# Dealing the steps of a prepared projection anew among the last slots of an attention loop

## The chip, the cores and the metric

The kernel runs on one core of a Trainium2 chip. A core has TensorE (PE; its weight loads are counted apart as PEld), VectorE (DVE), ScalarE (ACT), GpSimd (POOL) and SyncE (SP), whose queue issues nearly all transfers (DMAs) here. The metric is the device time of one execution in microseconds (us), the median of several. Beside it stands one execution recorded by the profiler. The kernel is a long one of some 1.37 milliseconds, with 36,810 recorded instructions.

## The reference

Four residual layers, A, B, A, B, on one sequence of 2048 rows of 512 numbers, in float32, with 32 heads of 16:

```python
def _A_ref(x, wqkv, w_phi, wo):          # linear attention with a softmax feature map
    q, k, v = ...                        # x @ wqkv, by heads
    phi_q, phi_k = ...                   # softmax(q @ w_phi) and softmax(-(q @ w_phi)), joined; k likewise
    kv = einsum("bhsf,bhsd->bhfd", phi_k, v); z = einsum("bhsf->bhf", phi_k)
    return (phi_q @ kv / (phi_q @ z + 1e-6)) @ wo

def _B_ref(x, wq, wk, wv, wo, beta):     # causal softmax attention in 4 segments of 512 rows, and a memory
    for s in range(4):
        p = softmax(qs @ ks.T * scale + mask)          # qs, ks, vs: segment s of q, k, v
        a_dot = p @ vs
        a_mem = phi(qs) @ M / (phi(qs) @ z + 1e-6)     # phi(t) = t + 1 where t > 0, else exp(t)
        outs.append(g * a_mem + (1 - g) * a_dot)       # g = sigmoid(beta)
        M, z = M + phi(ks).T @ vs, z + phi(ks).sum()
    return concat(outs) @ wo

x = x + _A_ref(layernorm(x), ...)        # twice: A, then B
x = x + _B_ref(layernorm(x), ...)
```

## The kernel before

**Precision.** Most matmuls split each factor into a high and a low part (the names end in h and l, so oh and ol are the parts of a transposed attention output o) and add up three products: high with high, high with low, low with high.

**The loop of a layer B.** `LayerB.steps` works off 32 half chunks: 4 segments, 4 chunks of 8 heads, and the two halves of a chunk. A half chunk has R = 5 slots, 0 to 4, so that "slot 7.3" is slot 3 of the eighth half chunk of a segment. The loop runs once per layer B. In each slot TensorE computes one piece of the attention scores (`attend`; tile lg, one buffer of two banks), ScalarE its exponential (tile P), and GpSimd masks the diagonal of P. Up to slot 6.0 of the last segment TensorE also computes the scores' maxima for a later half chunk (`maxima`; tiles mx, my, g). At slot 0 of the next half chunk `weighted` multiplies the probabilities with the values into g, and ScalarE copies the result to U; `finish` transposes U and weighs it into tmp or ot.

**The tables.** What else a slot does stands in a table of text: FIRST and GAPS for the segments 0 to 2, and for the last segment LAST in the first layer B and FINAL in the second. "7.2 P/5 v/1" means: in slot 7.2 take five steps of P and one of the work that follows the loop. A slot's own scores (and maxima) stand on TensorE ahead of what the table puts there. Within each engine instructions keep the order in which the program emits them (`held`, `Ordered`).

**P, the prepared projection.** `early` computes the output projection of the last segment for the first three of the four chunks, before the fourth is known: once for rows 0 and 1 of four blocks of 128 rows (slots 6.2 to 6.4), once for rows 2 and 3 (7.1 onward). "pre" loads the residual, "pt" transposes (o into oh and ol), and P takes steps of `mm3_pair`. What is left when the loop ends is run behind it, partly before `end_turn` transposes the last chunk and partly after; `end` then adds the fourth chunk's products and stores the result.

**`mm3_pair`.** It works two outputs at a time. TensorE's array is used as two halves of 64 rows; a step is two matmuls side by side, one per half, for two different banks (po). With three chunks there are 9 products, and the steps are dealt in three parts of 4, 9 and 5: steps 0 to 3, 4 to 12 and 13 to 17. Between two parts the row halves exchange the banks that they write. So that two halves do not write one bank at once, an empty instruction on SyncE's queue waits for the last matmul of the part, and the first matmul of the next part waits for that instruction. This is a handover; there are two per call, ahead of step 4 and of step 13. (With four chunks, as in Q, V and O, the parts have 6, 12 and 6 steps, and the tables deal those by sixes.)

**Buffers.** oh and ol have OO = 2 buffers each: the pair for rows 2 and 3 and then the pair of `end_turn`. So the parts that `end_turn` makes overwrite what the last steps of P read.

The order of TensorE is thus set by the tables alone. In LAST, slots 7.2 to 7.4 also hold "v", steps of the next layer A (a K projection: g<-e,hh and g<-e,hl).

Of the kernel before, what the change touches and what calls it, by code (L numbers as in the profile page):

```python
# [18 lines left out]
P = 128  # L19
# [60 lines left out]
3.0 max turn turn fin ln | 3.1 O/6     | 3.2 O/6           | 3.3 O/6 | 3.4 O/6  # L80
4.0 max ln ln a2 fin a2 | 4.1 v/2      | 4.2 v/2           | 4.3 v/2 | 4.4 v/2
5.0 max a3 a3 fin | 5.1 v/2           | 5.2 v/2           | 5.3 v/2 | 5.4 v/2
6.0 max fin pre | 6.1 pt pt         | 6.2 P/6           | 6.3 P/6 | 6.4 P/6 v/1
7.0 max pt pt fin | 7.1 P/4           | 7.2 P/5 v/1       | 7.3 P/5 v/1 | 7.4 P/4 v/2
"""
FINAL = """
0.0 max a1 a1 fin | 0.1 Q2/6          | 0.2 Q2/6          | 0.3 Q2/6 | 0.4 Q2/6
# [2 lines left out]
3.0 max a2 a2 fin | 3.1 O/6           | 3.2 O/6           | 3.3 O/6 | 3.4 O/6  # L90
4.0 max turn turn fin | 4.1 O/6        | 4.2 O/6           | 4.3 O/6 | 4.4 O/6
5.0 max a3 a3 fin | 5.1 O/6           | 5.2 O/6           | 5.3 O/6 | 5.4 O/6
6.0 max fin pre | 6.1 pt pt         | 6.2 P/6           | 6.3 P/6 | 6.4 P/6
7.0 max pt pt fin | 7.1 P/4           | 7.2 P/3           | 7.3 P/3 | 7.4 P/2
"""
BEFORE = {-25: "load q0", -24: "sq0 sq1", -23: "k0", -22: "sk0 n n", -21: "sk1 v0/2 n n", -20: "v0/2 n n",
          -19: "n n", -18: "v1 n n", -17: "q1/2", -16: "q1/2", -15: "k1/2", -14: "k1/2", -12: "max0", -11: "v2"}
# [1458 lines left out]
```

## Time and profile before

| | us |
|---|---|
| median of 3 runs | 1367.28 |
| lowest and highest run | 1366.54, 1372.07 |
| the profiled execution | 1365.67 |
| its span, first to last instruction | 1363.9 |
| TensorE busy (share of the span) | 1316.8 (97%) |
| VectorE, ScalarE, GpSimd busy | 1040.8, 808.6, 696.9 |
| mean granted TensorE clock | 0.997 |

The two loops of layer B end at about 697 us and 1352 us of the span. How to read a row of the timeline: start and duration in us, engine, line of the program, operation, the tile written and the tiles read, shapes, the number of equal instructions that the row merges, and in brackets how long the engine had been idle before it and what released it. "<-SPq" is SyncE's queue, "<-issue" a wait for which the profile shows no cause. Line 176 holds all matmuls, line 180 all transposes, line 154 all instructions of the other engines, so rows are told apart by their tiles. The row w,oh or w,ol into g is a step of P, where the shape says 64 rows; e,e into lg are scores; P,v into g are weighted values.

### The profile page before, as it was taken

To read this page: it belongs to the slowest core of one execution; us is meant where nothing else is said; L and a number is where in the kernel's file an instruction comes from. 1 tells how busy PE (TensorE), PEld (TensorE's weight loads), DVE (VectorE), ACT (ScalarE), POOL (GpSimd) and SP (SyncE) were. 2 spreads that over 40 slices of the span, in tenths; PEclk is the share of its full clock that TensorE was granted. 3 is DMA by queue.
4 is the path that set the end of the run, shared out by engine and by line. 5 is a ranking of instruction groups with operands and counts; after the bars stand their busy time and mean duration, and the time that the engine had idled before them with its cause. 6 is when DMAs were issued, how large, how long until landed. Compare 5 with 4: busy or idle time off the path is not lost.

```text
span 1363.9 us, 36810 instructions
## 1 busy us (share of the span) xinstructions
PE 1316.8 (97%) x14056; PEld 1030.0 (76%) x14056; DVE 1040.8 (76%) x3256; ACT 808.6 (59%) x1201; POOL 696.9 (51%) x1060
## 2 busy tenths in 40 slices
PE   7999989999999999999999998999999999999997
PEld 6888868767777777777668886886777787787764
DVE  4776778778888888888647677787778879878882
ACT  5556345547677677677544433463666866866654
POOL 1568666326447557345324356553356656654442
PEclk9999999999999999999999999999999999999999
DMA  6388447535554545546251103755556554544441
GB/s 204 101 320 276 163 129 231 168 103 141 166 170 133 156 118 134 154 119 180 87 177 41 63 32 125 233 163 139 138 161 171 148 159 101 147 130 100 118 113 45
DMA packets 134400, 196.27 MB, mean 144 GB/s; under 512 B 15440, under 2 KB 61648, under 8 KB 133456
## 3 DMA queue, kind: packets, MB, share of 16 engines
q1 hardware_dynamic: 132256, 193.27, 48.5%
q8 instruction: 112, 1.84, 0.5%
q10 hardware_dynamic: 1968, 0.64, 0.2%
q14 instruction: 64, 0.52, 0.1%
HBM read 101.05 MB, written 39.85 MB: 103 GB/s over the span
## 4 chain that ended last, share of the span: by engine, by line
PE 75%; DVE 11%; ACT 5%; issue 4%; POOL 3%; DMA 2%; SPq 1%; DVEq 0%; ACTq 0%; POOLq 0%
PE g L176 57%; PE lg L176 6%; PE g L180 6%; PE mx L176 3%; ACT P L154 2%; DVE g L154 2%; PE lg L180 2%; POOL P L154 1%; PE my L176 1%; POOL tb L154 1%; DVE my L154 1%; DVE mx L154 1%; DVE mxs L154 1%; DVE es L154 1%; PE mx L180 1%
## 5 line engine op out<-in xcount | busy, mean ns | idle before, releaser
L154 ACT ACTIVATE P<-lg 128x1024 f32<-128x1024 f32 x320 | 329.6, 1030 | 170.9 <-PE lg L176 93.1
L154 POOL TENSOR_SCALAR_AFFINE_SELECT P<-P 128x256 f32<-128x256 f32 (+1 forms) x448 | 193.4, 446 | 293.1 <-ACT P L154 292.6
L154 DVE CUSTOM_DVE_ANT_0 g<-g,mask 128x256 f32<-128x256 f32 (+3 forms) x392 | 191.7, 545 | 9.6 <-PE g L176 9.4
L176 PE MATMUL g<-hh,wqk 64*128 64x512 f32 (+1 forms) x960 | 186.8, 393 | 0.0
L176 PE MATMUL g<-w,oh 64*128 64x512 f32 (+2 forms) x880 | 177.7, 384 | 1.3 <-DVE ol L154 0.7
L154 DVE CUSTOM_DVE_ANT_0 mx<-mx,mask 128x512 f32<-128x512 f32 (+2 forms) x316 | 157.9, 500 | 24.1 <-PE my L176 14.4
L154 DVE CUSTOM_DVE_ANT_0 my<-my,mask 128x512 f32<-128x512 f32 (+2 forms) x316 | 164.2, 519 | 0.0
L176 PE MATMUL lg<-e,e 64*128 64x256 f32 (+2 forms) x1024 | 153.0, 339 | 4.1 <-ACT P L154 4.1
L176 PE MATMUL g<-P,v 128*32 128x128 f32 (+3 forms) x2064 | 151.1, 433 | 4.9 <-DVE mxs L154 4.3
L176 PE MATMUL g<-w,hh 64*128 64x512 f32 (+1 forms) x672 | 143.7, 395 | 2.3 <-ACT w L154 1.3
L154 DVE DVE_READ_ACCUMULATOR2_ANT mxs<- 128x1 f32 x1024 | 145.8, 142 | 0.0
L176 PEld LDWEIGHTS lg<-e,e 64*128 64x128 f32 x1024 | 102.0, 185 | 35.2 <-issue 11.3
L176 PEld LDWEIGHTS g<-P,v 128*32 128x32 f32 x2064 | 61.3, 109 | 88.8 <-issue 62.4
L176 PEld LDWEIGHTS g<-w,oh 64*128 64x128 f32 (+1 forms) x880 | 106.9, 186 | 18.4 <-SPq L154 2.8
L176 PEld LDWEIGHTS g<-hh,wqk 64*128 64x128 f32 (+1 forms) x960 | 105.8, 185 | 16.5 <-PE mx L176 0.7
L154 POOL TENSOR_SCALAR tb<-tb 128x512 f32<-128x512 f32 x72 | 109.1, 1527 | 16.0 <-ACT tb L154 16.0
L176 PE MATMUL g<-w,ol 64*128 64x512 f32 (+2 forms) x440 | 115.6, 377 | 0.5 <-DVE ol L154 0.5
L176 PE MATMUL g<-hl,wqk 64*128 64x512 f32 (+1 forms) x480 | 106.3, 391 | 0.2
L154 ACT COPY tb<-g 128x512 f32<-128x512 f32 (+1 forms) x132 | 71.1, 576 | 48.5 <-PE g L176 46.7
L176 PEld LDWEIGHTS g<-w,hh 64*128 64x128 f32 (+1 forms) x672 | 84.3, 188 | 16.9 <-ACT w L154 1.6
L176 PE MATMUL g<-w,hl 64*128 64x512 f32 (+1 forms) x336 | 90.1, 393 | 0.0
L154 DVE TENSOR_REDUCE es<-P 128x64 f32<-128x1024 f32 x64 | 77.4, 1209 | 12.8 <-ACT P L154 12.8
(149 smaller groups left out, 2888.7 us busy)
## 6 DMA issues: line engine op xcount, KB each, us to landing
e<-ta SPq DMA_DIRECT2D x384, 128.0 KB
wqk<-wqk SPq DMA_DIRECT2D x128, 256.0 KB
x<-x SPq DMA_DIRECT2D x48, 256.0 KB
ot<-in SPq DMA_DIRECT2D x26, 256.0 KB
pq<-tb SPq DMA_DIRECT2D x24, 256.0 KB
tb<-pq SPq DMA_DIRECT2D x24, 256.0 KB
x<-xr SPq DMA_DIRECT2D x22, 256.0 KB
xr<-x SPq DMA_DIRECT2D x20, 256.0 KB
```

Of the source, the lines that this page charges most:

```text
L154: i = f(*a, **k)
L176: return held(nc.tensor.matmul(*a, **k))
L180: return held(nc.tensor.transpose(*a))
```

## The change

Only the two tables that hold P are changed. In slots 6.2, 6.3 and 6.4 the steps go from 6, 6, 6 to 4, 9, 5, in both loops. In 7.1 to 7.4 the first loop goes from 4, 5, 5, 4 to 4, 5, 4, 5; in the second it goes from 4, 3, 3, 2 with six steps behind the loop to 4, 5, 4, 0 with five behind it.

```diff
@@ LAST
-6.0 max fin pre | 6.1 pt pt         | 6.2 P/6           | 6.3 P/6 | 6.4 P/6 v/1
-7.0 max pt pt fin | 7.1 P/4           | 7.2 P/5 v/1       | 7.3 P/5 v/1 | 7.4 P/4 v/2
+6.0 max fin pre | 6.1 pt pt         | 6.2 P/4           | 6.3 P/9 | 6.4 P/5 v/1
+7.0 max pt pt fin | 7.1 P/4           | 7.2 P/5 v/1       | 7.3 P/4 v/1 | 7.4 P/5 v/2
@@ FINAL
-6.0 max fin pre | 6.1 pt pt         | 6.2 P/6           | 6.3 P/6 | 6.4 P/6
-7.0 max pt pt fin | 7.1 P/4           | 7.2 P/3           | 7.3 P/3 | 7.4 P/2
+6.0 max fin pre | 6.1 pt pt         | 6.2 P/4           | 6.3 P/9 | 6.4 P/5
+7.0 max pt pt fin | 7.1 P/4           | 7.2 P/5           | 7.3 P/4 | 7.4
```

The change moves instructions on TensorE only. On the other four engines they stand in the same order before and after, as do the transfers. The places, as differences (minus before, plus after):

TensorE in the second loop, slots 6.2 and 6.3, around the first handover (the row that waits for SP_sequencer); g_20164 and g_20165 are the two banks of the prepared projection, lg the scores of 6.3:

```order
 L176 MATMUL g_20164<-w_14902,oh_20139 128x512
 L176 MATMUL g_20165<-w_14902,oh_20141 128x512
+L176 MATMUL lg_20175<-e_2263_12760,e_2264_12761 128x256 [waits Activation_49]
+L176 MATMUL lg_20175<-e_2263_12760,e_2264_12761 128x256
+L176 MATMUL lg_20175<-e_2263_12760,e_2264_12761 128x384 x2
 L176 MATMUL g_20165<-w_14902,oh_20141 128x512 [waits SP_sequencer_49]
 L176 MATMUL g_20164<-w_14902,oh_20139 128x512
 L176 MATMUL g_20165<-w_14903,oh_20141 128x512
 L176 MATMUL g_20164<-w_14903,oh_20139 128x512
-L176 MATMUL lg_20179<-e_2263_12760,e_2264_12761 128x256 [waits Activation_49]
-L176 MATMUL lg_20179<-e_2263_12760,e_2264_12761 128x256
-L176 MATMUL lg_20179<-e_2263_12760,e_2264_12761 128x384 x2
```

The scores of 6.3 moved ahead of steps 4 and 5, so that they stand between step 3 and the handover's wait; at 6.3 and 6.4 the scores of 6.4 likewise moved behind step 12, ahead of the wait of step 13.

TensorE in the first loop, slots 7.3 and 7.4; e,hh and e,hl are the work of the next layer A, lg the scores of 7.4:

```order
 L176 MATMUL g_10448<-w_4966,ol_10418 128x512
 L176 MATMUL g_10447<-w_4966,ol_10416 128x512
-L176 MATMUL g_10447<-w_4967,oh_10415 128x512 [waits SP_sequencer_49]
-L176 MATMUL g_10448<-w_4967,oh_10417 128x512
 L176 MATMUL g_10480<-e_1902_10380,hh_9449 128x512 [waits DMAHW7_49]
 L176 MATMUL g_10480<-e_1903_10381,hh_9449 128x512 [waits DMAHW0_49]
 L176 MATMUL g_10480<-e_1902_10380,hl_9450 128x512
-L176 MATMUL lg_10513<-e_450_2824,e_451_2825 128x256 [waits Activation_49]
-L176 MATMUL lg_10513<-e_450_2824,e_451_2825 128x256 x3
+L176 MATMUL lg_10511<-e_450_2824,e_451_2825 128x256 [waits Activation_49]
+L176 MATMUL lg_10511<-e_450_2824,e_451_2825 128x256 x3
+L176 MATMUL g_10447<-w_4967,oh_10415 128x512 [waits SP_sequencer_49]
+L176 MATMUL g_10448<-w_4967,oh_10417 128x512
```

Step 13, the one that waits for the handover, moved from behind step 12 to behind the next layer's products and the scores of 7.4.

TensorE behind the second loop, around the transposes of the last chunk (L180; tmp is the last attention output). Behind the loop came steps 12 to 15, these transposes, 16 and 17; now come 13 to 16, the transposes, and 17:

```order
 L176 MATMUL g_20280<-w_14902,oh_20248 128x512
 L176 MATMUL g_20281<-w_14902,oh_20250 128x512
-L180 MATMUL g_20390<-ident,tmp_19924 128x128 [waits DVE_49,PE_49]
-L180 MATMUL g_20390<-ident,tmp_19924 128x128
-L180 MATMUL g_20397<-ident,tmp_19924 128x128 [waits DVE_49,PE_49]
-L180 MATMUL g_20397<-ident,tmp_19924 128x128
 L176 MATMUL g_20280<-w_14903,oh_20248 128x512
 L176 MATMUL g_20281<-w_14903,oh_20250 128x512
+L180 MATMUL g_20392<-ident,tmp_19924 128x128 [waits DVE_49,PE_49]
+L180 MATMUL g_20392<-ident,tmp_19924 128x128
+L180 MATMUL g_20399<-ident,tmp_19924 128x128 [waits DVE_49,PE_49]
+L180 MATMUL g_20399<-ident,tmp_19924 128x128
```

The transposes of the last chunk moved behind step 16, the last one that reads an oh buffer. Ahead of it steps 7 to 12 moved forward: slot 7.2 held steps 4 to 6 and now 4 to 8, slot 7.3 held 7 to 9 and now 9 to 12, slot 7.4 held 10 and 11 and now none.

## The prediction

> **What bounds the kernel now.** I read the page's first table, then its costliest groups for what ends the idle time of the weight loads (PEld), then the timeline of TensorE and ScalarE at the places of the change. The rows of the page:
>
> ```profile
> PE 1316.8 (97%) x14056; PEld 1030.0 (76%) x14056; DVE 1040.8 (76%) x3256; ACT 808.6 (59%) x1201; POOL 696.9 (51%) x1060
> ...
> L176 PEld LDWEIGHTS g<-w,oh 64*128 64x128 f32 (+1 forms) x880 | 106.9, 186 | 18.4 <-SPq L154 2.8
> ```
>
> TensorE is busy for 97% of the span, so what the change can win is TensorE's time. The second row is the output projection, of which the prepared one is a part: in the whole run its weight loads stood idle for 2.8 us until SyncE's queue spoke. That is the handover between the row halves. The order of instructions has 128 waits of TensorE on SyncE, and this 2.8 us is what the change is after; it is 0.2% of the span and sets the scale.
>
> In the last layer's loop, slots 6.2 to 7.0. First the weight load behind the first exposed handover (step 4, in slot 6.2), then TensorE from 6.4 on, then ScalarE's exponentials of 6.3, 6.4 and 7.0:
>
> ```profile
> 1335.60 0.19 PEld L176 LDWEIGHTS g<-w,oh 64*128 64x128 f32 x2 [0.53 <-SPq L154]
> ```
> ```profile
> 1336.17 0.46 PE L176 MATMUL lg<-e,e 64*128 64x256 f32 x4
> 1336.47 0.40 PE L176 MATMUL g<-w,ol 64*128 64x512 f32 x2
> ...
> 1337.87 0.45 PE L176 MATMUL lg<-e,e 64*128 64x256 f32 x4
> 1338.15 0.39 PE L176 MATMUL g<-w,ol 64*128 64x512 f32 x2
> 1338.65 0.50 PE L176 MATMUL g<-w,oh 64*128 64x512 f32 x2
> 1338.98 0.40 PE L176 MATMUL g<-w,ol 64*128 64x512 f32 x2
> 1339.22 0.63 PE L176 MATMUL g<-w,oh 64*128 64x512 f32 x4
> 1339.68 0.39 PE L176 MATMUL g<-w,ol 64*128 64x512 f32 x2
> 1339.91 0.40 PE L176 MATMUL lg<-e,e 64*128 64x512 f32 x2
> ```
> ```profile
> 1336.73 1.03 ACT L154 ACTIVATE P<-lg 128x1024 f32<-128x1024 f32 x1 [1.75 <-PE lg L176]
> 1338.42 1.03 ACT L154 ACTIVATE P<-lg 128x1024 f32<-128x1024 f32 x1 [0.66 <-PE lg L176]
> 1340.41 1.02 ACT L154 ACTIVATE P<-lg 128x1024 f32<-128x1024 f32 x1 [0.97 <-PE lg L176]
> ```
>
> Steps 14 to 17 start at 1338.98, 1339.22 (two of them) and 1339.68, so a step in flow takes 0.70 / 3 = 0.233 us. From step 12 (1338.15) over step 13 (1338.65) to step 14 (1338.98) it is 0.83 in place of 0.47: **an exposed handover costs TensorE 0.36 us**, 0.26 as a wait and 0.10 since the next weights come late. ScalarE waits for TensorE before each of the three exponentials, so TensorE sets the pace here.
>
> **The change part by part.** All five terms are of moved TensorE instructions; nothing is added or removed, and the order of the other engines and of SyncE's queue is the same before and after. So no transfer is moved past another; what SyncE has behind a handover only gets free sooner.
>
> *Slots 6.2 to 6.4, in both loops.* The scores (lg) of 6.3 now follow step 3. They no longer stand behind two steps (0.47) and the stall (0.36), so they start at 1336.17 - 0.83 = 1335.34. Steps 4 to 12 follow 0.30 later (1336.17 to 1336.47 above): nine steps, 2.10 us. The handover needs 0.50 from the last step's start (1338.15 to 1338.65), and the step and the scores between cover 0.23 + 0.30 = 0.53; only the late weights may show, so I add 0.06. The scores of 6.4 start at 1335.34 + 0.30 + 0.06 + 2.10 = 1337.80, just 0.07 sooner than the 1337.87 above. Steps 13 to 17, again behind scores (0.28 + 0.06), would let the scores of 7.0 start at 1337.80 + 0.34 + 5 x 0.233 = 1339.31, 0.60 sooner than 1339.91. But the exponential of 6.4 is only 0.07 sooner: it ends at 1338.42 + 1.03 - 0.07 = 1339.38, and there is one score buffer. So the scores start near 1339.44 with late weights (0.10): the gain is 1339.91 - 1339.54 = **0.37 us**, not 0.60. Bounds: 0, if the scores' cover is too short and ScalarE takes the rest, and 0.72, both stalls. I take 0.37, as ScalarE's rows stand nearest. Cover gone, each handover would cost its 0.36 again. What follows in 7.0 and 7.1 hangs on TensorE and passes this on. The first loop has the same two slots in the same order, and its part of the 2.8 us (six stalls of 0.47 on the mean, two each in these slots of both loops) says that they stall alike. So 0.37 twice.
>
> *Slot 7.3 of the first loop.* TensorE, where a piece of the next layer's K projection (g<-e,hh and hl; "v/1") follows the prepared steps 12 and 13:
>
> ```profile
> 692.21 0.39 PE L176 MATMUL g<-w,ol 64*128 64x512 f32 x2
> 692.70 0.50 PE L176 MATMUL g<-w,oh 64*128 64x512 f32 x2
> 693.13 0.73 PE L176 MATMUL g<-e,hh 128*128 128x512 f32 x2
> 693.70 0.40 PE L176 MATMUL g<-e,hl 128*128 128x512 f32 x1
> 694.02 0.52 PE L176 MATMUL lg<-e,e 64*128 64x256 f32 x4
> ```
>
> Step 13 moves behind the scores of 7.4. The handover is then covered by the K projection and the scores, over 1.2 us. A step followed by another kind of work takes about 0.32 (the second of the two steps at 1349.53 below starts at 1349.76, what follows at 1350.08), so the K projection starts at about 692.53, the scores at 693.42 in place of 694.02; the moved step (0.23) comes back in 7.4. Net **0.37 us**; bounds 0.26 (the wait alone) and 0.49 (692.70 less 692.21).
>
> *Slots 7.2 to 7.4 of the last loop.* TensorE in 7.2 and 7.4, then the mask (affine select) on the last probabilities:
>
> ```profile
> 1346.08 0.63 PE L176 MATMUL g<-w,oh 64*128 64x512 f32 x4
> 1346.54 0.40 PE L176 MATMUL g<-w,ol 64*128 64x512 f32 x2
> 1347.42 0.39 PE L176 MATMUL lg<-e,e 64*128 64x256 f32 x2 [0.48 <-ACT P L154]
> ```
> ```profile
> 1349.53 0.62 PE L176 MATMUL g<-w,oh 64*128 64x512 f32 x4
> 1350.08 2.37 PE L176 MATMUL g<-P,v 128*32 128x256 f32 x48
> ```
> ```profile
> 1350.90 0.64 POOL L154 TENSOR_SCALAR_AFFINE_SELECT P<-P 128x512 f32<-128x512 f32 x1 [0.94 <-ACT P L154]
> ```
>
> Here scores and exponential take turns at one buffer, and TensorE idles. From 1346.08 to 1347.42 there are 1.34 us; five steps take 1.17, so two more cost nothing (0.17 is left; with that cover gone, each further step costs 0.23). Slot 7.3 goes from three steps to four, with more to spare. Slot 7.4 loses its two steps, and the weighted sums need not wait until 1350.08. They are 48 instructions in 12 passes of four, about 0.2 each, and the last pass of all takes 0.4 to end. The last two passes read probabilities whose mask ends at 1350.90 + 0.64 = 1351.54, and they now start near 1350.08 + 2.37 - 0.4 - 0.2 = 1351.85. With 0.05 to 0.1 from mask to TensorE the gain is **0.2 us**, bounds 0 and 0.3.
>
> *Behind the last loop.* TensorE, ScalarE's cast and VectorE's low half:
>
> ```profile
> 1353.47 0.49 PE L176 MATMUL g<-w,ol 64*128 64x512 f32 x2
> 1354.07 0.50 PE L176 MATMUL g<-w,oh 64*128 64x512 f32 x2
> 1354.40 0.40 PE L176 MATMUL g<-w,ol 64*128 64x512 f32 x2
> 1354.63 0.39 PE L176 MATMUL g<-w,oh 64*128 64x512 f32 x2
> 1354.95 0.66 PE L180 MATMUL g<-ident,tmp 128*128 128x128 f32 x4
> 1355.54 0.50 PE L176 MATMUL g<-w,oh 64*128 64x512 f32 x2
> ```
> ```profile
> 1356.08 0.65 ACT L154 CAST oh<-g 128x256 fp32r<-128x256 f32 x2 [3.02 <-PE g L176]
> ```
> ```profile
> 1354.26 0.29 DVE L154 TENSOR_TENSOR tmp<-tmp,wt 128x128 f32<-128x128 f32 x1
> 1356.48 0.76 DVE L154 TENSOR_TENSOR ol<-g,oh 128x256 fp32r<-128x256 f32 x2 [1.93 <-ACT oh L154]
> ```
>
> Steps 12 to 15 stand at 1353.47 to 1354.63, the last transposes at 1354.95, then step 16, and 17 behind it. The cast writes the buffer (OO = 2) that step 16 reads: step 16 ends at 1355.54 + 0.50 = 1356.04, and the cast starts at 1356.08, though all four transposes had ended at 1354.95 + 0.66 = 1355.61. Afterwards four steps are left ahead of the transposes, 13 to 16: 1353.47, then 0.33 and twice 0.23 on, then 0.32 (1354.63 to 1354.95) to the transposes at 1354.59 (VectorE's tmp ends at 1354.55: just in time for the second pair). Step 17 follows 0.59 later (1354.95 to 1355.54 above) at 1355.18 and ends at 1355.68. The cast needs only its transposes, near 1355.1, so VectorE's low half, which overwrites what step 17 reads, starts at 1355.72 in place of 1356.48: **0.76 us**, more than the stall itself. Bounds 0.36 and 1.0. Everything behind it, to the last stores, hangs on it.
>
> Sum: 0.37 + 0.37 + 0.37 + 0.2 + 0.76 = 2.07, about 2.1 us. The profiled execution took 1365.67 (span 1363.9 and 1.8 around it), 1.6 below the median of 1367.28; it would come to 1363.6, and the median to 1365.2.
>
> **Rivals.**
>
> *The cover is too short (the change does not do what it says).* In 6.2 to 7.0 only 0.28 to 0.30 of scores stand in the border, and nine steps in 6.3 hold back the exponential of 6.4. If these slots win nothing in both loops, 1.33 is left: 1366.0. For it: the margin is 0.03 us. Against: even then the scores of 6.4 are not later than now.
>
> *The half clock.* In the second layer's first pass, the chain of waits and the windows around it:
>
> ```profile
> 836.85 2.23 issue
> ```
> ```profile
> 840.00:844.00 4.00, 4.00 (x12) 3.05 (x11) 3.93 (x7) 0.00 (x0) 2.33 (x3) 0.58 0.87 299
> ```
>
> TensorE waits 2.23 us for nothing that the trace names, and in the next 4 us its granted clock is 0.58, which costs 0.42 x 4 = 1.7 us. The first loop's 0.74 us moves the idle stretch; if the drop follows from where the stretch lies in a fixed grid, it can go, and the time is 1363.5. Against: nothing says so but one drop. [...]
>
> *One more such wait (slower).* The same "issue" wait, and the half clock behind it, cost 2.23 + 1.7 = 3.9 us. If moving TensorE's work by 0.74 us makes one more of them, say where the second layer's weights are loaded, the time is 1365.2 + 3.9 = 1369.1. It decides from 2.1 us on. For it: it is there once, in a stretch with DMA busy for 0.87. Against: instructions and transfers move together.
>
> **How the numbers follow.** The forecast has 0.55 (its own range, each term halfway to its bounds, is 1.3 to 2.7 us: 1364.6 to 1366.0). Too short a cover has 0.2, the clock 0.1, one more wait 0.1, other ways 0.05. The runs shown lie between 1366.54 and 1372.07, so 0.5% (6.8 us) is about what a measurement tells from no change. No case reaches it: same 0.95, slower 0.03, faster 0.02 for what no row shows. The range is 1361.8 to 1369.2: the clock's case less the forecast's spread, up to one more wait.
>
> **What would show it.** Right: no weight load of the output projection waits for SyncE; the scores of 6.3 start some 0.8 us sooner after those of 6.2, those of 6.4 about as now, and the exponential of 7.0 0.4 sooner; the cast behind the last loop starts ahead of step 17's end, and from the last U to the end the time is 0.8 shorter. Wrong: waits on SyncE of some 0.1 to 0.4 at 6.3 and 6.4, scores of 7.3 that come late behind five steps, or a last cast that waits as long as now.

## The result and the profile after

The changed kernel took 1362.78 us (median of 22 runs), the kernel before 1365.37 us beside it (22 runs): a ratio of 0.9974 with a 95% interval of 0.9963 to 0.9985, or 3.5 us less (2.0 to 5.0); the two medians by themselves lie 2.6 apart. Two of the changed kernel's 22 executions took 2557.12 and 4822.27 us, at a granted clock of 1.0; the ratio is without them, and why they took so long is open. The change is within 0.5%, as forecast, and by the ratio some 1.4 us more than the forecast 2.1. A later comparison of the same two kernels on one chip (below) gave 0.9989 (0.9973 to 1.0006), some 1.5 us less, with an interval that includes 1.

The profiled execution of the changed kernel took 1367.52 us, *more* than the 1365.67 of before. Its mean granted clock was 0.991, against 0.997, and its TensorE waited 0.50 and 0.53 us for SyncE at two places that the change does not touch (g<-hh,wqk, at 351.08 and 453.17). The changed places have to be read by themselves, then, as distances within one trace.

The page of the changed kernel, TensorE and the weight loads of the output projection:

```profile
PE 1320.3 (97%) x14056; PEld 1036.5 (76%) x14056; DVE 1041.6 (76%) x3256; ACT 808.2 (59%) x1201; POOL 695.2 (51%) x1060
...
L176 PEld LDWEIGHTS g<-w,oh 64*128 64x128 f32 (+1 forms) x880 | 108.9, 187 | 15.0 <-issue 1.5
```

The 2.8 us that these loads waited for SyncE's queue are gone: what ends most of their idle time is no longer "SPq", and the longer list of what they waited for in this trace does not name it.

The last loop, slots 6.2 to 7.0 in the changed kernel; TensorE at the two handovers, then ScalarE's exponentials of 6.2, 6.3, 6.4 and 7.0:

```profile
1337.98 0.73 PE L176 MATMUL g<-w,oh 64*128 64x512 f32 x2
1338.32 0.68 PE L176 MATMUL lg<-e,e 64*128 64x256 f32 x4
1338.80 0.73 PE L176 MATMUL g<-w,oh 64*128 64x512 f32 x4
...
1340.76 0.39 PE L176 MATMUL g<-w,ol 64*128 64x512 f32 x2
1340.99 0.40 PE L176 MATMUL lg<-e,e 64*128 64x256 f32 x4
1341.26 0.50 PE L176 MATMUL g<-w,oh 64*128 64x512 f32 x2
```
```profile
1337.13 1.04 ACT L154 ACTIVATE P<-lg 128x1024 f32<-128x1024 f32 x1
1339.09 1.03 ACT L154 ACTIVATE P<-lg 128x1024 f32<-128x1024 f32 x1 [0.92 <-POOL P L154]
1341.50 1.02 ACT L154 ACTIVATE P<-lg 128x1024 f32<-128x1024 f32 x1 [1.37 <-PE lg L176]
1343.17 1.02 ACT L154 ACTIVATE P<-lg 128x1024 f32<-128x1024 f32 x1 [0.65 <-PE lg L176]
```

Both handovers now have scores in them: from the last step (1340.76) over the scores (1340.99) to the next step (1341.26) is 0.50, the time that a handover took before, and TensorE works through it. The cover is only just as long as the handover. The row of 6.3 names GpSimd's mask (POOL P) as what released the exponential. The end of the scores, 1338.32 + 0.68 = 1339.00, explains its start as well: it comes 0.09 later, as in the kernel before (1336.17 + 0.46 = 1336.63, then 1336.73 at TensorE's release). Whether the mask too would hold it back is not shown. The kernel before had its exponential of 6.2 here, and its last U further on:

```profile
1333.94 1.04 ACT L154 ACTIVATE P<-lg 128x1024 f32<-128x1024 f32 x1
...
1352.58 0.47 ACT L154 ACTIVATE U<-g,share 128x256 f32<-128x256 f32 x1 [1.02 <-PE g L176]
```

From the exponential of 6.2 to those of 6.3, 6.4 and 7.0 it was 2.79, 4.48 and 6.47 us; it is 1.96, 4.37 and 6.04. So 6.3 comes 0.83 sooner, 6.4 only 0.11 and 7.0 0.43.

The first loop, slot 7.3 in the changed kernel: TensorE, where the next layer's K projection stands between step 12 and the scores of 7.4, then ScalarE's exponentials of 7.3 and 7.4 and its U behind the loop:

```profile
692.54 0.63 PE L176 MATMUL g<-w,oh 64*128 64x512 f32 x4
693.10 0.73 PE L176 MATMUL g<-e,hh 128*128 128x512 f32 x2
693.67 0.40 PE L176 MATMUL g<-e,hl 128*128 128x512 f32 x1
694.00 0.56 PE L176 MATMUL lg<-e,e 64*128 64x256 f32 x4
```
```profile
694.69 1.03 ACT L154 ACTIVATE P<-lg 128x1024 f32<-128x1024 f32 x1 [1.54 <-PE lg L176]
696.95 1.03 ACT L154 ACTIVATE P<-lg 128x1024 f32<-128x1024 f32 x1 [1.24 <-PE lg L176]
...
701.96 0.69 ACT L154 ACTIVATE U<-g,share 128x512 f32<-128x512 f32 x1 [2.57 <-PE g L176]
```

The same rows of the kernel before:

```profile
691.81 1.03 ACT L154 ACTIVATE P<-lg 128x1024 f32<-128x1024 f32 x1 [1.55 <-PE lg L176]
694.66 1.03 ACT L154 ACTIVATE P<-lg 128x1024 f32<-128x1024 f32 x1 [1.82 <-PE lg L176]
...
699.41 0.69 ACT L154 ACTIVATE U<-g,share 128x512 f32<-128x512 f32 x1 [2.32 <-PE g L176]
```

From 7.3 to 7.4 it was 2.85 and is 2.26; from 7.3 to U it was 7.60 and is 7.27.

The last weighted sums of the changed kernel: GpSimd's last mask, then the weight loads of the last passes:

```profile
1353.67 0.63 POOL L154 TENSOR_SCALAR_AFFINE_SELECT P<-P 128x512 f32<-128x512 f32 x1 [0.94 <-ACT P L154]
```
```profile
1354.36 0.16 PEld L176 LDWEIGHTS g<-P,v 128*32 128x32 f32 x8 [0.52 <-POOL P L154]
```

The mask ends at 1354.30, and these loads, now early, wait 0.52 for it; in the kernel before the 48 loads ran in one stretch of 1.89 us, from 1350.08 on.

Behind the last loop of the changed kernel: TensorE's transposes and step 17, ScalarE's last U and the cast, VectorE's low half:

```profile
1357.16 0.66 PE L180 MATMUL g<-ident,tmp 128*128 128x128 f32 x4
1357.74 0.50 PE L176 MATMUL g<-w,ol 64*128 64x512 f32 x2
```
```profile
1355.13 0.47 ACT L154 ACTIVATE U<-g,share 128x256 f32<-128x256 f32 x1 [1.16 <-PE g L176]
1357.63 0.65 ACT L154 CAST oh<-g 128x256 fp32r<-128x256 f32 x2 [2.03 <-PE g L180]
```
```profile
1358.35 0.76 DVE L154 TENSOR_TENSOR ol<-g,oh 128x256 fp32r<-128x256 f32 x2 [1.24 <-PE g L176]
```

The cast now waits for the transposes (line 180) and starts 2.50 behind the last U rather than 3.50. VectorE's low half waits for step 17 (line 176), no longer for the cast alone, and starts 3.22 behind the last U rather than 3.90. (In some traces of the same order, that of experiment 7 among them, its row names the cast, with 1.24 us of idle time as here; experiment 6 settles that it is the buffer.)

### The profile page after: what moved, and what is told of

It is laid out like the page before. It is cut to its first block, busy times and chain, and to the rows that moved or that the text cites. A ratio compares the mean times of both kernels' runs of the same rounds, so it can differ in the third digit from the quotient of the medians.

```text
span 1365.7 us, 36810 instructions
## 1 busy us (share of the span) xinstructions
PE 1320.3 (97%) x14056; PEld 1036.5 (76%) x14056; DVE 1041.6 (76%) x3256; ACT 808.2 (59%) x1201; POOL 695.2 (51%) x1060
## 4 chain that ended last, share of the span: by engine, by line
PE 74%; DVE 11%; ACT 4%; issue 4%; POOL 3%; DMA 2%; SPq 1%; DVEq 0%; ACTq 0%; POOLq 0%
PE g L176 56%; PE lg L176 6%; PE g L180 5%; PE mx L176 3%; ACT P L154 2%; PE lg L180 2%; POOL P L154 2%; DVE g L154 2%; SPq L154 1%; DVE es L154 1%; POOL tb L154 1%; PE my L176 1%; DVE my L154 1%; DVE mx L154 1%; DVE mxs L154 1%
```

## The experiments

Experiments 1 to 7 are one execution each, and their whole times, 1363.29 to 1367.30 us, tell nothing at this scale. Their expectations were written with the changed kernel's trace known, and quote it in places; what they left open was which part of the change does what. Their verdicts rest on six distances, each worked out from two starts in one trace (us). A: first loop, exponential of 6.2 to that of 7.0. B: first loop, exponential of 7.3 to U. C: as A, in the last loop. D: exponential of 7.0 to the last U. E: last U to the cast. F: last U to VectorE's low half. From there to the end it is 7.37 to 7.40 in every trace.

| | A | B | C | D | E | F |
|---|---|---|---|---|---|---|
| before | 6.48 | 7.60 | 6.47 | 12.17 | 3.50 | 3.90 |
| before, again | 6.47 | 7.63 | 6.47 | 12.17 | 3.50 | 3.90 |
| after | 6.34* | 7.27 | 6.04 | 11.96 | 2.50 | 3.22 |
| after, again | 6.04 | 7.27 | 6.04 | 11.95 | 2.50 | 3.21 |
| 1: slots 6.2 to 6.4 alone | 6.06 | 7.59 | 6.04 | 12.17 | 3.51 | 3.91 |
| 2: 7.2 to 7.4 of the last loop alone | 6.47 | 7.60 | 6.47 | 11.94 | 2.50 | 3.21 |
| 3: 7.3 and 7.4 of the first loop alone | 6.77* | 7.25 | 6.46 | 12.16 | 3.51 | 3.91 |
| 4: three steps in each of 7.2 to 7.4 | 6.37* | 7.24 | 6.03 | 12.40 | 2.50 | 3.21 |
| 5: before, free buffers | 6.77* | 7.59 | 6.46 | 12.17 | 2.86 | 3.26 |
| 6: after, free buffers | 6.05 | 7.25 | 6.04 | 11.94 | 2.50 | 2.90 |
| 7: 4, 6 and 8 steps | 6.12 | 7.27 | 6.13 | 11.94 | 2.50 | 3.22 |
| 8: free buffers, one step moved back | 6.05 | 7.27 | 6.04 | 11.95 | 2.26 | 2.67 |

The star marks stretches 0.29 to 0.33 longer than in the other traces of the same order. In that of "after" the granted clock was 0.50 for a part, from 678.31 to 681.73 (see the last section); I put the other three down to the same. Without those, one place repeats to within 0.05 us, mostly 0.02, whatever else was changed. So differences of 0.1 us can be told here, though the runs' times scatter by several us.

**1. Slots 6.2 to 6.4 alone.** The kernel before with one row of each table changed:

```diff
-6.0 max fin pre | 6.1 pt pt         | 6.2 P/6           | 6.3 P/6 | 6.4 P/6
+6.0 max fin pre | 6.1 pt pt         | 6.2 P/4           | 6.3 P/9 | 6.4 P/5
```

> Only the rows of slots 6.2 to 6.4 are changed (4, 9, 5 steps), in both loops. By the forecast's terms the scores of 6.3 come 0.83 us sooner after the exponential of 6.2, the exponential of 6.4 0.07 to 0.11 sooner, that of 7.0 0.37 to 0.43 sooner, in each loop; the slots 7.x and the work behind the last loop lie as before, so VectorE's low half (ol) still stands behind a cast that ends near where it did, and the whole is 0.7 to 0.9 us. Rival, the cover is too short: waits of the weight loads on SyncE of 0.1 to 0.4 us show at 6.3 and 6.4, and the exponential of 7.0 comes no sooner.

A and C fell by 0.42 and 0.43, all else stayed. ScalarE in the last loop (6.2, 6.3, 6.4, 7.0) and what ended the idle time of the weight loads:

```profile
1333.32 1.04 ACT L154 ACTIVATE P<-lg 128x1024 f32<-128x1024 f32 x1
1335.28 1.02 ACT L154 ACTIVATE P<-lg 128x1024 f32<-128x1024 f32 x1 [0.92 <-POOL P L154]
1337.69 1.02 ACT L154 ACTIVATE P<-lg 128x1024 f32<-128x1024 f32 x1 [1.38 <-PE lg L176]
1339.36 1.02 ACT L154 ACTIVATE P<-lg 128x1024 f32<-128x1024 f32 x1 [0.65 <-PE lg L176]
```
```profile
  SPq L154: 0.9, 2
```

Two long waits on SyncE are left, those at the first loop's 7.3 and behind the last loop. The scores do cover a handover, and the rival of too short a cover falls: the exponential of 7.0 comes 0.43 sooner with these rows alone.

**2. Slots 7.2 to 7.4 of the last loop alone.**

```diff
-7.0 max pt pt fin | 7.1 P/4           | 7.2 P/3           | 7.3 P/3 | 7.4 P/2
+7.0 max pt pt fin | 7.1 P/4           | 7.2 P/5           | 7.3 P/4 | 7.4
```

> Only the row of slots 7.2 to 7.4 of the last loop is changed (5, 4, 0 steps). By the forecast's terms the exponentials of 7.1 to 7.4 keep their distance to each other, the last weighted sums end 0.2 us sooner, the cast behind them starts a further 0.9 to 1.0 sooner and VectorE's low half (ol) 0.76 sooner (0.68 in the changed kernel), together 0.9 to 1.0 us to the end; the stalls in 6.2 to 6.4 stay. Rival, the gain behind the loop needs the earlier slots too (the steps there run later because 7.0 is later): under 0.5 us to the end.

D fell by 0.23, E by 1.00 and F by 0.69: 0.92 to the end, as expected, with the stalls of 6.2 to 6.4 still there. The gain does not need the earlier slots.

**3. Slots 7.3 and 7.4 of the first loop alone.** The LAST row of the change, 4 and 5 steps in place of 5 and 4.

> Only slots 7.3 and 7.4 of the first loop are changed (4 and 5 prepared steps). By the forecast's terms the scores and the exponential of 7.4 come 0.6 us sooner after those of 7.3, the moved step takes 0.23 back in 7.4, and what follows the loop is 0.37 us sooner (0.33 in the changed kernel). Rival, the moved step brings a new stall in 7.4 or the K projection waits for its own handover: 0.1 or less is left behind the loop.

The exponential of 7.4 came 2.25 behind that of 7.3 rather than 2.85, and B fell by 0.35. No new stall came with the moved step.

**4. Which steps stand ahead of the last weighted sums.** The changed kernel, with the same number left behind the loop:

```diff
-7.0 max pt pt fin | 7.1 P/4           | 7.2 P/5           | 7.3 P/4 | 7.4
+7.0 max pt pt fin | 7.1 P/4           | 7.2 P/3           | 7.3 P/3 | 7.4 P/3
```

> As the changed kernel, but the last loop's slots 7.2 to 7.4 hold 3, 3 and 3 steps in place of 5, 4 and none, so that the same four steps are left behind the loop and the same handover is avoided there. If the gain behind the loop comes from which step the cast waits for, the time from the last weighted sums to VectorE's low half is as in the changed kernel (0.7 us shorter than before); the three steps ahead of the weighted sums of 7.4 hold these back by one step more than before, 0.2 us later than before and 0.4 to 0.5 later than in the changed kernel. Rival, the weighted sums are bound by the mask of the last probabilities alone, wherever the steps stand: no later than in the changed kernel by more than 0.1.

E and F are those of the changed kernel, 2.50 and 3.21; D is 12.40, that is 0.23 later than before and 0.45 later than in the changed kernel. The rival, that the mask alone sets the weighted sums, falls. So the two parts come apart: the gain behind the loop comes from how many steps are left there, the gain in D from where the others stand. One more step ahead of the weighted sums costs one step, 0.23.

**5 and 6. Is it the buffer?** The parts of `end_turn` go to the buffers of ta1, which are free behind both loops, in the kernel before and in the changed one:

```diff
-    def turn(ot):
+    def turn(ot, tags=(("oh", OO), ("ol", OO))):
-        o = [T2("oh", OO, F32R), T2("ol", OO, F32R)]
+        o = [T2(tag, bufs, F32R) for tag, bufs in tags]
-            return [turn([last[:, t], last[:, t + 1]]) for t in (0, 2)]
+            return [turn([last[:, t], last[:, t + 1]], (("ta1", TA),) * 2) for t in (0, 2)]
```

> The kernel before, but the two parts of the result behind the last loop are written to free buffers (those of ta1) rather than to those of oh and ol that the prepared steps 16 and 17 still read; all steps stand as before. If it is the buffer that holds back the cast, it starts when its four transposes have ended: 0.5 to 0.65 us sooner after the last weighted sums than before, and VectorE's low half with it, whose wait is then for the cast alone; the exposed handover between steps 12 and 13 stays. Rival, the cast waits for TensorE's order and not for the buffer: nothing moves.

In the kernel before, with not one step moved, the last U, the cast and VectorE's low half:

```profile
1354.16 0.47 ACT L154 ACTIVATE U<-g,share 128x256 f32<-128x256 f32 x1 [1.02 <-PE g L176]
1357.02 0.65 ACT L154 CAST ta<-g 128x256 fp32r<-128x256 f32 x2 [2.39 <-PE g L180]
```
```profile
1357.42 0.76 DVE L154 TENSOR_TENSOR ta<-g,ta 128x256 fp32r<-128x256 f32 x2 [1.29 <-ACT ta L154]
```

The cast's wait is now for line 180, the transposes, and E and F fell by 0.64 each. The buffer was what held it back. Of the 1.00 that the change takes off E, 0.64 is the buffer; the other 0.36 (2.86 to 2.50 with free buffers, experiment 6) is the price of the handover that is no longer exposed.

> The changed kernel, but with the free buffers behind the last loop. In the changed kernel the cast starts at its transposes' end already, and VectorE's low half waits for step 17. Without that wait the cast lies as in the changed kernel, and VectorE's low half follows it 0.4 us after its start rather than 0.72: 0.3 us sooner to the end. Rival, the cast too still waited for step 16: then it comes sooner by some 0.1 to 0.3.

VectorE's low half in the changed kernel with free buffers:

```profile
1355.84 0.76 DVE L154 TENSOR_TENSOR ta<-g,ta 128x256 fp32r<-128x256 f32 x2 [0.93 <-ACT ta L154]
```

E stayed at 2.50 and F fell by 0.31 to 0.32, to 0.40 behind the cast. So in the changed kernel the low half's buffer still cost 0.3.

**7. Where the second handover lies.** The changed kernel with 4, 6 and 8 steps in slots 6.2 to 6.4 of both loops, which puts the second handover back inside slot 6.4.

> The changed kernel, but slots 6.2 to 6.4 of both loops hold 4, 6 and 8 steps rather than 4, 9 and 5. The first handover lies behind the scores of 6.3 as in the changed kernel, the second inside slot 6.4 as before (its wait of 0.4 to 0.5 on SyncE shows again). By the forecast's arithmetic the scores of 6.4 come three steps (0.7 us) sooner than in the changed kernel, the exponential of 6.4 as soon as ScalarE is free, and the scores of 7.0 stand behind all 18 steps and one stall: the exponential of 7.0 is 0.1 us later than in the changed kernel if TensorE sets it (0.83 of stalls less 0.36), or as in it. Rival, the exponential of 6.4 was what held up 7.0, so that bringing it forward by 0.7 us pays: the exponential of 7.0 is 0.2 us or more sooner than in the changed kernel.

The weight load behind that handover, then the exponentials of 6.4 and 7.0:

```profile
1337.25 0.19 PEld L176 LDWEIGHTS g<-w,oh 64*128 64x128 f32 x2 [0.53 <-SPq L154]
```
```profile
1336.57 1.03 ACT L154 ACTIVATE P<-lg 128x1024 f32<-128x1024 f32 x1 [0.68 <-PE lg L176]
1339.02 1.02 ACT L154 ACTIVATE P<-lg 128x1024 f32<-128x1024 f32 x1 [1.42 <-PE lg L176]
```

The stall is back, and A and C are 6.12 and 6.13: 0.34 to 0.36 less than before, 0.08 or 0.09 more than in the changed kernel. The exponential of 6.4 came 0.7 us sooner than there and gained nothing, since TensorE then had its stall ahead of 7.0. One covered handover is worth the 0.36 that an exposed one costs; covering the second brings only 0.08 more. The rival, 0.2 us or more sooner than in the changed kernel, falls. In the changed kernel it is ScalarE's exponential of 6.4 that then holds back the scores of 7.0, as their weight load shows:

```profile
1342.57 0.19 PEld L176 LDWEIGHTS lg<-e,e 64*128 64x128 f32 x2 [0.32 <-ACT P L154]
```

**8. A version that takes both.** The changed kernel with free buffers and one of the steps behind the loop back in slot 7.4:

```diff
-7.0 max pt pt fin | 7.1 P/4           | 7.2 P/5           | 7.3 P/4 | 7.4
+7.0 max pt pt fin | 7.1 P/4           | 7.2 P/5           | 7.3 P/4 | 7.4 P/1
-            for _ in range(4):
+            for _ in range(3):
```

> The changed kernel with the free buffers, and with one of the steps behind the last loop moved back to slot 7.4, so that three stand ahead of the last transposes. By the forecast's arithmetic the weighted sums are not later (they wait for the mask), the transposes 0.2 us sooner, the cast with them and VectorE's low half 0.4 behind it: 0.4 to 0.5 us less than the changed kernel to the end, about 2.5 to 4 us under the kernel before, a ratio of 0.997 to 0.998. Rival, the transposes wait for VectorE's tmp and not for the steps: the step moved brings nothing, 0.3 less than the changed kernel.

```profile
1353.31 0.47 ACT L154 ACTIVATE U<-g,share 128x256 f32<-128x256 f32 x1 [1.03 <-PE g L176]
1355.58 0.68 ACT L154 CAST ta<-g 128x256 fp32r<-128x256 f32 x2 [1.79 <-PE g L180]
```

The weighted sums are no later for the step (D is 11.95, and 11.96 in the changed kernel), the cast is 0.24 sooner, and F falls to 2.67, 0.55 less than in the changed kernel. In its trace this version is 2.6 us faster than the kernel before at the changed places. Its median was 1362.81 (12 runs) against 1365.30 (17 runs), a ratio of 0.9978 (0.9964 to 0.9991), an interval that leaves out 1. That it beats the changed kernel is seen in the trace alone; the runs' scatter does not tell 0.5 us.

**9 and 10. The two kernels again, on one chip.**

> The kernel before, unchanged, in five rounds beside itself. It shows how far two sets of runs of one kernel on one chip differ, and how a run's time goes with its mean granted clock: the ratio is 1 within 0.1%, and 0.001 of clock is 1 to 1.4 us if the half clock alone makes the spread.

> The changed kernel in five rounds beside the kernel before, on the same chip. Theory: at the same clock it is 2 us faster (the traces' landmarks: 1.3 in the last loop and behind it, 0.7 to 1.1 in the first), and what it wins beyond that in the medians is chance of the half clock. Rival: the change makes the half clock rarer, so that its mean clock is higher by 0.001 or more and the ratio 0.9974 or below.

The kernel before gave 1366.50 (23 runs), the same program beside it 1365.31 (12 runs), a ratio of 0.9993 (0.9978 to 1.0008), so two sets of one kernel differ by 1.2 us in the median. The changed kernel gave 1364.89 (12 runs), 0.9989 (0.9973 to 1.0006): by the times alone no difference is shown here. A straight line for time against mean granted clock, with an offset for the kernel, through these 47 runs has a slope of -1.2 us per 0.001 of clock and an offset of -1.7 us, plus or minus 0.9 (95%). At equal clock the changed kernel is faster, then, by an amount that agrees with 2.1. The rival, a clock higher by 0.001 or more, is not seen: on this chip the mean clock was 0.9960 for the kernel before (35 runs) and 0.9957 for the changed one (12), and over all larger sets, of several chips, 0.9959 (52 runs) and 0.9960 (32), a difference that is known to 0.0008 either way (95%).

## Why the prediction was right

- **Slots 6.2 to 6.4, 0.37 in each loop.** Measured 0.42 to 0.44 where the clock was full. The inner steps came out as forecast: the scores' exponential of 6.3 sooner by 0.83 (forecast 0.83), that of 6.4 by 0.11 (0.07), that of 7.0 by 0.43 (0.37, and not the 0.60 that TensorE alone would have allowed). The 0.06 that I added for late weights was about 0.04 too much.
- **Slot 7.3 of the first loop, 0.37.** Measured 0.33 to 0.35.
- **Slots 7.2 to 7.4 of the last loop, 0.2.** Measured 0.21 to 0.23. The five steps in 7.2 hid behind ScalarE: in experiment 2 every exponential from 7.0 to 7.4 stands 0.55 or 0.56 us ahead of its place in the kernel before; that all are shifted alike means that none came later to the others. The weighted sums now wait for the mask, as the row of 1354.36 shows, 0.06 behind its end (forecast 0.05 to 0.1). Their slack shows in experiment 8, where a step ahead of them cost nothing, while three cost 0.45 in experiment 4.
- **Behind the last loop, 0.76.** Measured 0.68 or 0.69. The mechanism, the buffer, was right; the size was off by the 0.1 us between step 17's end (1357.74 + 0.50 = 1358.24) and VectorE's start (1358.35), which I had set at 0.04.
- **The sum, 2.07.** Measured 0.44 + 0.33 + 0.43 + 0.22 + 0.69 = 2.11 between the profiles of before and of "after, again".
- **The median, 1365.2; measured 1362.78.** This is the step that was off: I put the sum on the median of the three runs shown, 1367.28, though I had noted that the profiled execution lay 1.6 below it. Over 22 runs the median of before is 1365.37, and 2.1 less is 1363.3; the other 0.5 us is less than two sets of one kernel differ by. That the median came so near to this is in part luck: the two comparisons put the gain at 3.5 and 1.5 us. So is its place in the range. The lower bound of 1361.8 does not follow from the words beside it, since the clock's case less the forecast's spread is 1363.5 - 0.6 = 1362.9, and 1362.78 lies just below that.
- **The rivals.** Too short a cover fell in experiment 1. The half clock is there in both kernels: before, the granted clock was 0.50 from 20.78 to 24.19 and from 839.98 to 843.39; after, for 3.41 or 3.42 us from 19.54, 278.96, 678.31, 842.16 and 944.56 and for 6.83 from 179.97. Over all larger sets the mean clocks are alike (experiments 9 and 10), so nothing here shows that it went away or came with the change. "One more issue wait" did not happen in the traces: in the second layer's first pass TensorE waits once, as before, in the changed kernel's trace here:

```profile
841.25 0.46 PE L176 MATMUL my<-v,P 128*32 128x17 f32 x33 [1.93 <-issue]
```

What is not shown: that all of the first loop's 0.77 us reaches the end. Between the loops the clock differs from trace to trace, by more than that: before, it was 0.50 there once for 3.41 us, after twice, and a stretch with TensorE busy throughout loses about 0.5 x 3.41 = 1.7 us by it (an estimate from these two traces). The offset of 1.7 plus or minus 0.9 at equal clock leaves it open.

## What to carry to other kernels

A wait of half a microsecond is worth moving to where the engine has other work anyway; but its price is read at what follows, here 0.36 us per exposed handover, and covering two in a row paid little more than covering one, since the next engine (ScalarE with one score buffer) took over as the limit. Look at what the last transposes and casts overwrite: free buffers alone gave nearly as much behind the loop, 0.64 us, as moving the steps, 0.69. Where a change is below the scatter of runs, compare distances between fixed instructions in the traces, which repeated to 0.05 us here, and put a forecast on many runs' median, not on three.

## What was not expected of the hardware

In the profiled executions of before and after the granted clock was 0.50 for stretches of 3.41 or 3.42 us, once for 6.83: two of them before, six after. Two of those in the changed kernel's trace, each below the 3.41 or 3.42 us ahead of it (busy time of the engines, granted clock, DMA share):

```profile
core 0: us, PE busy (x) PEld busy (x) DVE busy (x) ACT busy (x) POOL busy (x), PEclk, DMA share, GB/s
674.90:678.31 3.41, 2.14 (x16) 1.17 (x12) 0.97 (x4) 2.12 (x4) 1.24 (x3) 1.00 0.00 0
678.31:681.73 3.42, 3.42 (x17) 2.97 (x18) 1.02 (x2) 1.89 (x3) 1.05 (x3) 0.50 0.01 5
838.74:842.16 3.42, 1.49 (x103) 1.32 (x93) 1.77 (x3) 2.41 (x3) 2.35 (x3) 1.00 0.99 340
842.16:845.57 3.41, 3.41 (x9) 2.65 (x9) 3.34 (x6) 0.00 (x0) 2.61 (x3) 0.50 1.02 355
```

And the same place as the second of them in the trace of "after, again":

```profile
839.23:842.64 3.41, 1.78 (x39) 1.53 (x40) 2.67 (x6) 1.53 (x2) 2.11 (x3) 1.00 1.05 380
842.64:846.06 3.42, 2.54 (x16) 1.94 (x14) 3.32 (x6) 1.38 (x2) 1.41 (x2) 1.00 0.71 240
```

With TensorE busy for 1.49 of 3.42 us the clock was 0.50 in what followed; with 1.78 of 3.41 it stayed at 1.00. In the kernel before it was 0.50 at this place too, from 839.98 to 843.39, behind 1.18 of 3.41 us busy. Idle time just ahead doesn't settle it, as the first pair shows: TensorE was idle there for 37% of 3.41 us and the half clock followed, while behind the 48% of "after, again" it did not. The half clock from 678.31 on fell on slots 6.2 to 6.4 of the first loop and lowered what the change won there from 0.44 to 0.14 (A in the table).

What brings the half clock, and whether it follows from where an idle stretch lies, as the forecast's rival supposed, is not shown. What is shown is that the same program has it at a place in one execution and not in the next, and how much of the difference between runs goes with the mean granted clock: the line through the 47 runs accounts for about three quarters of the spread in their times. That the change could shift the half clock for good was the forecast's rival; the mean clocks of 0.9959 before and 0.9960 after (known to 0.0008 either way) show no such shift.
